# A Fourier filter and memory attention on one core: low parts a unit later, a first projection unit without butterflies, triangle zeros split around the maxima, other pacing and load times

## The chip, the core and the metric

The kernel runs on one core of one Trainium2 chip. The metric is device microseconds of one execution. Where the profile speaks of engines, PE is the matrix engine (TensorE), PEld its weight loads, DVE VectorE, ACT ScalarE, POOL GpSimd, and SP the engine that issues most DMAs.

## The reference, cut to what matters

Two unrelated problems share the kernel; their outputs are concatenated.

```
# A: x [1,2048,576], 32 heads of 18, four segments of 512 tokens
q,k,v = heads(x@wq), heads(x@wk), heads(x@wv)
for s in range(4):
    p = softmax(qs@ks.T*18**-0.5 + causal_mask);  a_dot = p@vs
    a_mem = (phi(qs)@M) / (phi(qs)@z + 1e-6)      # memory of earlier segments
    outs.append(g*a_mem + (1-g)*a_dot)
    M += phi(ks).T@vs;  z += sum(phi(ks))
a = concat(outs)@wo
# B: x [1,2048,576]
b = irfft2(rfft2(x) * (w_r + 1j*w_i))
```

## The kernel before, in words

Every engine has one queue, worked off in the order in which the Python code emits instructions; there is no reordering by a scheduler (`manual_schedule`). An instruction that waits holds up all that stands behind it on its engine. Numbers in f32 are split into a high part (a rounded copy) and a low part (the rest), and products are summed over the parts, so that a matmul has companions on ACT (copy of the high part) and DVE (subtraction for the low part).

The program has four stages on PE, which the trace shows one after the other: the forward transform of B, the projections of A, the inverse transform of B, and attention with the output projection.

**Forward transform** (`FFT.forward`). There are 16 units. For a unit u: SP loads `xin` (L114, three buffers); DVE makes sum and difference `eo` (L126, two instructions, two buffers); ACT copies them to the high part `eh` (L129, L130, three fixed tiles); DVE subtracts for the low part `el` (L133). `f1(u)` is 14 matmuls (L145) into one of two PSUM buffers, eight on `eh`, four on `el` and two on a mixed tile, each half starting with four on `eh`. ACT copies the result to `X0` (L150), DVE subtracts for `X1` (L153), and only then is the PSUM buffer free for `f1(u+2)`. `c1(u)` is 12 matmuls (L166) on `X0`, `X1` and a matrix `cfw` that POOL's queue loads (L118, four buffers); ACT copies its result to the array `Z` (L157). In the loop at step u PE gets `f1(u)` and `c1(u-2)`; DVE gets `eo(u+2)`, a subtraction for a projection weight (L429, called `wl` below), `X1(u-1)` and `el(u+2)`. In the first steps `X1` stands ahead of `eo`.

**Projections** (`ATT.projections`). Four segments, each with nine units of queries and keys and four of values. A query/key unit is 14 matmuls of 512 columns (L485) into one of five PSUM buffers `pj`. What follows is a chain over three engines: ACT copies the first bf16 part `sp` (L498), DVE subtracts it from PSUM (L505), ACT copies the second part (L512), PE subtracts that with one matmul (L514, weights `nid`), ACT copies the third part (L515). PE's queue has the L514 of a unit behind the 14 matmuls of the next unit. On DVE and ACT the same stage carries pieces of the middle of the transform: butterflies on `Z` (L230) and twiddles (`tw` on ACT, L239, then L242 on DVE). A counter (`Pace`) hands them out: `take(w)` per unit, with `w` worked out from how many pieces are left.

**Attention** (`ATT.attention`). A step t is one head; four steps make a block k. In step t PE computes the scores of head t+11 once to find row maxima (`s1`, L678, maxima on DVE at L686 and L692), the scores of head t a second time with the maximum subtracted (`s2`, L727 to L736), ACT takes the exponential into `P` (L728, L733, L737), and PE multiplies an earlier block with the values (`pv`, L756: in step 4k+5 the first half of block k, in step 4k+7 the second). The zeros above the diagonal are written by POOL after the block's last head: four `affine_select` instructions at L741, of about 0.6 us each, on the tiles P0, P1 (twice) and P2. The first half of `pv` reads P0 and the last quarter of P1; the second half reads the rest of P1 and P2. `mpath(k+2)` begins in step 4k+4: DVE (L704) and ACT (L705) finish the maxima of a later block, POOL splits them into two bf16 parts `mh` (L707, L708), and one step later PE transposes them (L711, tile `mt`).

The rest of attention's work stands in a background list `bg`: preparation of the output weights (`late_setup`; its subtraction `wol` on POOL is L650), the denominators (`den`), then per segment `mixed` (memory product `pn` at L831, broadcasts `pb` at L837 and L878, their use on DVE at L838, L881, L883, an addition on POOL at L884) and the output projection `oproj` (L901). `pn` and `pb` share one PSUM buffer. `run_bg` is called twice a step, with 0 and with 1.2: it adds the number to an account and runs one piece when the account is at least 1. So at 1.2 every fifth step runs two pieces.

Loads for later steps go through a list `q`, from which a step takes one (every eighth step two). In steps 16 to 20 five tiles `pq` of 252 or 144 KB are loaded as well, for `den` in step 34. ACT's queue issues one small DMA per block, which brings the maxima to the query tile (L717).

Of the kernel before, what the change touches and what calls it, by code (L numbers as in the profile page):

```python
# [5 lines left out]
F32=mybir.dt.float32; F32R=mybir.dt.float32r  # L6
# [96 lines left out]
class FFT:  # L103
# [4 lines left out]
    def forward(s,xp,cp,pp,wl,xs,consts):  # L108
# [3 lines left out]
        def load(u):  # L112
            xin[u]=xp.tile([128,2,3,128],F32,name="xin",bufs=3)
            nc.sync.dma_start(xin[u],io["xb"][u])  # L114
        def loadc(u):
            a,b=BORD[u]
            cw[u]=cp.tile([128,2,384],F32R,name="cfw",bufs=4)
            nc.gpsimd.dma_start(cw[u],io["cfw"][4*a+b].rearrange("p (h m) -> p h m",h=2))  # L118
# [65 lines left out]
        for i in range(2):  # L184
            for x in p: next(x)
        load(3)
        zp=pp.tile([128,2,512],F32,name="f1",tag="f1")
        zeros(26)
        s.pace=Pace(44+124+32)
        for u in range(20):  # L190
            p=prep(u+2) if u+2<16 else iter(())
            if 0<u<17: ev0(u-1)
            if 2<u<18: evz(u-3)
            if 0<u<4: ev1(u-1)
            if u%4==3 and u>6: s.pace.add(s.stage1((u-7)//4))
            next(p,None)
            if 1<u: next(wl,None)
            if 3<u<17: ev1(u-1)
            next(p,None)
            if u<16: f1(u)  # L200
            if u+4<16: load(u+4)
            elif u<18: next(xs,None)
            if 1<u<18: c1(u-2)
            if u==17: evz(15)
            if 0<u<15: loadc(u+1)
            if u>13: s.pace.take(2)
# [201 lines left out]
class ATT:  # L408
# [58 lines left out]
    def first(s,x0,xp):  # L467

        s.xh={};s.xl={}; s.x0=x0
        P=[s.xprep(0,t,x0,xp,[128,2,3,128],"xin",3) for t in range(5)]  # L470
# [100 lines left out]
    def projections(s,xp,tp,pp,wv,pace,hook):  # L571

        live=[]
        s.nid=wv.tile([128,128],BF,name="nid"); s.nc.scalar.activation(s.nid,s.ident,AF.Copy,scale=-1.0)
        lw=s.load_w("wv",576,wv,xp,288,"xl",4)
        def advance():
            for l in list(live):
                try: next(l)
                except StopIteration: live.remove(l)
        tot=pace.left-8  # L580
        for g in range(4):
            if g<3: xq=[s.xprep(g+1,t,(xp,s.x0)[g%2],xp,[128,512],"xst",2) for t in range(5)]
            for i in range(13):
                u=s.qk_unit(g,i,tp,pp) if i<9 else s.v_unit(g,i-9,tp,pp)
                if i==4 and g<3: s.pk=tp.tile([128,4,576],F32,name="pk",bufs=1)
                next(u)
                hook(g,i)
                next(lw,None); next(lw,None)
                if g<3 and i in (4,6,8,10,12): next(xq[(i-4)//2])
                if g<3 and i in (1,3,5,7,9): next(xq[(i-1)//2])  # L590
                w=tot/(36+16*2.4)*(1.0 if i<9 else 2.4)
                advance()
                pace.take(w*.4)
                advance()
                next(u)
                pace.take(w*.6)
                live.append(u)
        while live: advance()
# [34 lines left out]
    def late_setup(s,cp):  # L633
# [4 lines left out]
        for t in (0,1,2,3,5,4,6):  # L638
# [6 lines left out]
            if len(q)>(t<6):  # L645
# [3 lines left out]
                nc.scalar.copy(s.woh[:,u],x)  # L649
                nc.gpsimd.tensor_tensor(s.wol[:r,u],x[:r],s.woh[:r,u].bitcast(F32),op=OP.subtract)  # L650
        yield
# [67 lines left out]
    def s2(s,t):  # L719
# [19 lines left out]
        if hh==3 or k==31 and hh==2:  # L739
            def sel(x):  # L740
                nc.gpsimd.affine_select(out=x[:,r],in_=x[:,r],pattern=[[0,r.stop-r.start],[1,128]],compare_op=OP.is_ge,fill=0.0,base=0,channel_multiplier=-1)  # L741
            sel(P[0][:,:,:128])
            sel(P[1][:,:,:128])
            sel(P[1][:,:,384:])
            sel(P[2][:,:,:128])
        yield
# [94 lines left out]
    def mixed(s,g):  # L841

        c=s.combine(g-1)
        d=5 if g==3 else 4
        for i in range(5+d):
            next(c,None); yield
            if i>=d:
                for _ in s.mem1(g,ORD[i-d]): yield
    def ux_load(s,g,t):
        r=126 if t<4 else 72  # L850
        s.ux[t]=s.tp.tile([128,512],F32,name="ux",tag="ux",bufs=3)
        s.nc.sync.dma_start(s.ux[t][:r],s.uD[g][126*t:126*t+r])
    def combine(s,g):
# [19 lines left out]
        for t in range(7+late):  # L873
            if t>1 and not late: high(ORD[t-2]); low(ORD[t-2])
            if t<5:
# [6 lines left out]
                else:  # L882
                    nc.vector.tensor_tensor(x[:r],x[:r],pb[:r],op=OP.mult)  # L883
                    eng().tensor_tensor(s.am[t][:r],x[:r],s.am[t][:r],op=OP.add)  # L884
                t=i
# [53 lines left out]
    def begin(s,sm,sp,ps1):  # L939
        s.late=[]; s.now=-1  # L940
        s.sm,s.sp,s.ps1=sm,sp,ps1
        s.mh=sm.tile([128,8,16],BF,name="mh",bufs=1); s.nc.gpsimd.memset(s.mh,0.0)
        s.mg={};s.mx={};s.m2={};s.P={};s.vs={};s.rc={};s.am={};s.pq={};s.ux={};s.potag=None
    def prologue(s):
# [20 lines left out]
    def attention(s,tp,ps):  # L965
# [7 lines left out]
        q=[]  # L973
# [11 lines left out]
        for t in range(133):  # L985
            k,hh=divmod(t,4); n,qd=divmod(k,2); g=k//8
            if hh==0 and qd==0:
                if 0<n<14: q+=s.stack_dmas(n+2,0)
                if 0<n<13: q+=s.stack_dmas(n+3,1)
                if n+2<16: q.append(lambda n=n: s.load_v(n+2))  # L990
            st=t%32
            if 16<=t<21: s.pq_load(1,ORD[t-16])
            if t==34: bg.append(s.den(1,lane))
# [187 lines left out]
```

## Time and profile before

| | |
|---|---|
| median of 3 runs | 700.23 us (699.89 to 700.64) |
| the profiled execution | 701.5 us, its span 699.8 us |
| PE busy | 680.0 us (97%), 5040 matmuls |
| DVE, ACT, POOL busy | 537.7 us (77%), 445.3 us (64%), 192.3 us (27%) |
| chain that ended last | PE 83%, DVE 6%, DMA 3%, ACT 3%, POOL 2%, issue 2% |
| granted TensorE clock | 1.00 |
| DMA | 123.81 MB, mean 177 GB/s |

The span is the time from the first to the last instruction of the trace. A row of a timeline gives the start and the length in us, then the engine, the line, the operation, and what it writes and reads; a number in square brackets is the idle time of the engine just before it, with what ended that time. Matmuls are pipelined: one of 512 columns on f32 is shown as some 400 ns long and yet the next starts after some 230 ns, so rows of PE overlap. A row of the waits gives the total in us, how often, and the longest.

### The profile page before, as it was taken

The page shows a single profiled execution, that of the slowest core. Times are in us where ns is not written, and L with a number is a line of the kernel's source. Part 1 is how long each engine was busy: PE and PEld are TensorE (multiplying, and loading weights), DVE is VectorE, ACT ScalarE, POOL GpSimd, SP SyncE. Part 2 cuts the span into 40 slices and gives each one's busy share as a digit, 9 for nine tenths or more (in the row PEclk, how much of TensorE's full clock was granted, in tenths as well). Part 3 has the DMA queues.
Part 4 walks back from the last instruction along what each step waited for, and adds up shares of the span by engine and source line. Part 5 has one row for each costly group of instructions (what it writes and reads, how often), then busy time and mean ns, then how long its engine had stood idle before and what let it go on. Part 6 is the DMA issues. An engine that isn't in the chain of part 4 may idle for free.

```text
span 699.8 us, 14371 instructions
## 1 busy us (share of the span) xinstructions
PE 680.0 (97%) x5040; PEld 501.9 (72%) x5040; DVE 537.7 (77%) x1149; ACT 445.3 (64%) x997; POOL 192.3 (27%) x389
## 2 busy tenths in 40 slices
PE   8999899999999999999999899999999999998998
PEld 5999679879879879999954455445666445663497
DVE  5898989789689679798588788888667876567633
ACT  4786695584684574545387687777656776567531
POOL 2111000100200101665135343443323652235310
PEclk9999999999999999999999999999999999999999
DMA  9895355594465778999348876986666776442142
GB/s 335 279 316 179 111 162 190 154 268 155 130 191 190 171 213 297 206 231 250 130 124 193 182 172 153 197 196 161 148 141 166 200 161 154 101 132 67 29 152 90
DMA packets 71362, 123.81 MB, mean 177 GB/s; under 512 B 12236, under 2 KB 39530, under 8 KB 67698
## 3 DMA queue, kind: packets, MB, share of 16 engines
q1 hardware_dynamic: 64638, 106.89, 58.0%
q0 software_dynamic: 5632, 15.76, 8.3%
q8 instruction: 40, 0.66, 0.4%
q10 hardware_dynamic: 1020, 0.25, 0.2%
q14 instruction: 32, 0.26, 0.1%
HBM read 82.10 MB, written 39.81 MB: 174 GB/s over the span
## 4 chain that ended last, share of the span: by engine, by line
PE 83%; DVE 6%; DMA 3%; ACT 3%; POOL 2%; issue 2%; ACTq 0%; SPq 0%; DVEq 0%; POOLq 0%
PE pj L485 15%; PE s L678 10%; PE pv L756 10%; PE pjv L485 9%; PE po L901 6%; PE i L318 4%; PE i L329 4%; PE s L727 3%; PE f L145 3%; PE s L731 3%; PE c L166 3%; PE po L930 2%; PE s L691 2%; PE pn L831 2%; PE pm L553 2%
## 5 line engine op out<-in xcount | busy, mean ns | idle before, releaser
L686 DVE CUSTOM_DVE_ANT_0 junk<-s,x 128x512 bf16<-128x512 f32 x248 | 137.0, 552 | 56.0 <-PE s L678 50.9
L741 POOL TENSOR_SCALAR_AFFINE_SELECT P<-P 128x512 f32<-128x512 f32 (+2 forms) x132 | 78.2, 623 | 112.4 <-ACT P L728 104.6
L692 DVE TENSOR_REDUCE mx<-s 128x4 f32<-128x512 f32 x128 | 87.7, 685 | 6.2 <-PE s L691 3.9
L728 ACT ACTIVATE P<-s 128x512 f32<-128x512 f32 x128 | 77.9, 609 | 12.3 <-PE s L727 3.4
L756 PE MATMUL pv<-P,vs 128*32 128x512 f32 (+3 forms) x1024 | 82.5, 439 | 0.1
L737 ACT ACTIVATE P<-s 128x256 f32<-128x256 f32 x128 | 50.0, 391 | 46.3 <-PE s L736 46.0
L733 ACT ACTIVATE P<-s 128x512 f32<-128x512 f32 x128 | 77.8, 608 | 2.5 <-PE s L732 2.2
L678 PE MATMUL s<-Ks,Qs 108*128 108x384 bf16 (+3 forms) x256 | 69.2, 301 | 1.5 <-DVE mx L692 1.2
L756 PEld LDWEIGHTS pv<-P,vs 128*32 128x32 f32 x1024 | 26.9, 109 | 45.3 <-issue 34.9
L485 PE MATMUL pj<-x,wqkh 128*128 128x512 f32 x162 | 56.4, 408 | 0.0
L230 DVE TENSOR_TENSOR Z<-Z 128x580 f32<-128x580 f32 (+2 forms) x51 | 45.6, 911 | 0.5
L678 PEld LDWEIGHTS <-Qs 108*128 108x128 bf16 x320 | 31.5, 98 | 19.3 <-issue 9.2
L691 PE MATMUL s<-tri,idb 128*128 128x128 bf16 x256 | 43.0, 219 | 0.0
L543 POOL MEMSET vt<- 128x32 f32 x16 | 2.3, 161 | 139.1 <-PE pm L553 127.8
L318 PE MATMUL i<-civ,Y 128*128 128x256 f32 (+1 forms) x288 | 39.2, 288 | 0.2 <-POOL Y L303 0.2
L318 PEld LDWEIGHTS i<-civ,Y 128*128 128x128 f32 (+1 forms) x288 | 36.6, 181 | 0.9 <-POOL Y L303 0.4
L329 PE MATMUL i<-itab,T 128*128 128x290 f32 (+1 forms) x224 | 36.6, 306 | 0.1
L485 PEld LDWEIGHTS pj<-x,wqkh 128*128 128x128 f32 x162 | 30.4, 189 | 8.5 <-issue 2.0
L485 PE MATMUL pj<-xh,wqkl 128*128 128x512 f32 x90 | 35.6, 395 | 0.0
L485 PE MATMUL pj<-xh,wqkh 128*128 128x512 f32 x90 | 35.6, 395 | 0.0
L485 PE MATMUL pj<-x,wqkl 128*128 128x512 f32 x90 | 35.5, 395 | 0.0
L504 DVE SCALAR_TENSOR_TENSOR ex<-pj,ex 128x512 f32<-128x512 f32 (+1 forms) x28 | 19.3, 689 | 20.2 <-ACT ex L502 20.1
(216 smaller groups left out, 1805.9 us busy)
## 6 DMA issues: line engine op xcount, KB each, us to landing
qkD<-sp SPq DMA_DIRECT2D x32, 384.0 KB
xin<-xb SPq DMA_DIRECT2D x16, 384.0 KB
cfw<-cfw POOLq DMA_DIRECT2D x16, 384.0 KB, 5.5
civ<-civ POOLq DMA_DIRECT2D x16, 384.0 KB, 9.7
vs<-vD SPq DMA_DIRECT2D x16, 330.0 KB
vD<-vt SPq DMA_DIRECT2D x16, 311.0 KB
W<-w SPq DMA_DIRECT2D x16, 290.0 KB
yb<-yout SPq DMA_DIRECT2D x16, 290.0 KB
```

Source lines behind the costliest of these rows:

```text
L318: nc.tensor.matmul(p[:m,k],Y[i][:,q,c*128:c*128+m],cc[:,hl,o:o+256],start=n==0,stop=n==5)
L329: nc.tensor.matmul(p,x,t,start=n==0,stop=n==6)
L485: s.nc.tensor.matmul(out,a,b,start=i==0,stop=i==len(L)-1)
L678: nc.tensor.matmul(out,Q[:108,h,128*i:128*i+128],K[:108,h,:128*(i+1)],start=True,stop=True)
L686: nc.vector.tensor_tensor_reduce(out=junk[:,:w],in0=src,in1=s.mask[:,512-w:],scale=1.0,scalar=-3.0e38, op0=OP.add,op1=OP.max,accum_out=s.m ...
L691: nc.tensor.matmul(pa[:,o+w-128:o+w],s.idb,s.tri,start=False,stop=True,skip_group_check=True)
L692: nc.vector.tensor_reduce(out=s.mx[k][:,hh],in_=pa.rearrange("p (b c) -> p b c",c=128),axis=mybir.AxisListType.X,op=OP.max)
L728: nc.scalar.activation(P[0][:,hh],p0,AF.Exp,scale=SC)
L733: nc.scalar.activation(P[1][:,hh],p1,AF.Exp,scale=SC)
L737: nc.scalar.activation(P[2][:,hh],p2,AF.Exp,scale=SC)
L741: nc.gpsimd.affine_select(out=x[:,r],in_=x[:,r],pattern=[[0,r.stop-r.start],[1,128]],compare_op=OP.is_ge,fill=0.0,base=0,channel_multiplie ...
L756: nc.tensor.matmul(s.pvt[32*hh:32*hh+32,128*j:],vt[:,j,19*h:19*h+32],mv[0][:,hh,mv[1]],start=j==0,stop=j>1,skip_group_check=True)
```

## The change

The edits fall in three groups.

- *Forward.* `xin` has four buffers and `cfw` three. In step u DVE now gets `eo(u+2)`, `wl`, `X1(u-1)` and then `el(u+1)`, the low part of the unit made in the step before; in the first steps too `X1` stands ahead of `el`.
- *Projections.* The first unit of the first segment takes no pieces (`w` is 0 there); the others get a little more each, and five pieces instead of eight are left for later.
- *Attention.* POOL writes P0 and the last quarter of P1 in step 4k+3, and P1's first quarter and P2 in step 4k+4 behind the two `mh` instructions. The `wol` subtraction and, in steps of one kind, the addition of `combine` go to the end of their step. The background rate is 1.2 at first, 1.0 while `mixed` of segments 1 and 2 runs, 1.35 after it, and 1.2 from `mixed` of segment 3 on. The five `pq` loads stand in steps 18, 21, 24, 27 and 30; the load of the values is put at place 6 of the list `q` instead of its end.

```diff
-            xin[u]=xp.tile([128,2,3,128],F32,name="xin",bufs=3)
+            xin[u]=xp.tile([128,2,3,128],F32,name="xin",bufs=4)
...
-            cw[u]=cp.tile([128,2,384],F32R,name="cfw",bufs=4)
+            cw[u]=cp.tile([128,2,384],F32R,name="cfw",bufs=3)
...
+        p=[]
...
-            p=prep(u+2) if u+2<16 else iter(())
+            if u+2<16: p.append(prep(u+2))
             if 0<u<17: ev0(u-1)
             if 2<u<18: evz(u-3)
-            if 0<u<4: ev1(u-1)
             if u%4==3 and u>6: s.pace.add(s.stage1((u-7)//4))
-            next(p,None)
-            if 1<u: next(wl,None)
-            if 3<u<17: ev1(u-1)
-            next(p,None)
+            if u>=2:
+                if u<14: next(p[-1])
+                next(wl,None)
+            if 0<u<17: ev1(u-1)
+            if 0<u<15: next(p.pop(0))
+            if u<2: next(p[-1])
             if u<16: f1(u)
...
-        tot=pace.left-8
+        tot=pace.left-5
...
-                w=tot/(36+16*2.4)*(1.0 if i<9 else 2.4)
+                w=tot/(35+16*2.4)*((1.0 if i<9 else 2.4) if g>0 or i>=1 else 0.0)
...
-                nc.gpsimd.tensor_tensor(s.wol[:r,u],x[:r],s.woh[:r,u].bitcast(F32),op=OP.subtract)
+                s.later(1,lambda u=u,x=x,r=r: nc.gpsimd.tensor_tensor(s.wol[:r,u],x[:r],s.woh[:r,u].bitcast(F32),op=OP.subtract))
+                yield
...
             sel(P[0][:,:,:128])
-            sel(P[1][:,:,:128])
             sel(P[1][:,:,384:])
-            sel(P[2][:,:,:128])
+            def rest():
+                sel(P[1][:,:,:128])
+                sel(P[2][:,:,:128])
+            if k<31: s.rest=rest
+            else: rest()
...
+        s.rate=1.0 if g<3 else 1.2
         c=s.combine(g-1)
...
+        if g<3: s.rate=1.35
...
-                    eng().tensor_tensor(s.am[t][:r],x[:r],s.am[t][:r],op=OP.add)
+                    f=lambda t=t,x=x,r=r,e=eng(): e.tensor_tensor(s.am[t][:r],x[:r],s.am[t][:r],op=OP.add)
+                    f() if eng() is nc.vector or s.now%4<3 or g==2 else s.later(1,f)
...
-                if n+2<16: q.append(lambda n=n: s.load_v(n+2))
+                if n+2<16: q.insert(6,lambda n=n: s.load_v(n+2))
             st=t%32
-            if 16<=t<21: s.pq_load(1,ORD[t-16])
+            if t in (18,21,24,27,30): s.pq_load(1,ORD[(18,21,24,27,30).index(t)])
...
-            run_bg(1.2)
+            run_bg(s.rate)
...
             if hh==0 and k+2<32: m=s.mpath(k+2); next(m)
+            if hh==0 and s.rest: s.rest(); s.rest=None
```

Three places show how this moves instructions. The numbers in tile names count allocations. In the changed file lines stand 2 to 9 lower (L431 is the old L429, L507 the old L505, L744 the old L741).

DVE in the forward transform, from the sum and difference of unit 2 on, before: each `el` stands right behind the `eo` of its own unit (`eh` names ACT's copy in between).

```order
L126 TENSOR_TENSOR eo_189<-xin_132 128x384 x2
L133 TENSOR_TENSOR el_194<-eo_189,eh2_114 128x768
L153 TENSOR_TENSOR X1_220<-f1_196,X0_218 128x580
L126 TENSOR_TENSOR eo_222<-xin_160 128x384 x2
L133 TENSOR_TENSOR el_227<-eo_222,eh0_112 128x768
L153 TENSOR_TENSOR X1_250<-f1_229,X0_248 128x580
L126 TENSOR_TENSOR eo_252<-xin_216 128x384 x2
```

And in the changed kernel, from the same instruction on:

```order
L126 TENSOR_TENSOR eo_189<-xin_132 128x384 x2
L153 TENSOR_TENSOR X1_218<-f1_194,X0_216 128x580
L133 TENSOR_TENSOR el_220<-eo_189,eh2_114 128x768
L126 TENSOR_TENSOR eo_222<-xin_160 128x384 x2
L126 TENSOR_TENSOR eo_248<-xin_214 128x384 x2
L153 TENSOR_TENSOR X1_257<-f1_227,X0_246 128x580
L133 TENSOR_TENSOR el_259<-eo_222,eh0_112 128x768
```

Between an `eo` and its `el` there now stand another unit's `eo` and an `X1`; `X1` of unit 1 (X1_257) stands behind the `eo` of units 3 and 4, where it had stood ahead of the latter (X1_250).

ACT at the start of the projections, before; `sp3` are the parts of the first units (1015, 1044, 1087 are units 0, 1, 2), `wvh` a value weight, `tw` the twiddles of a butterfly stage.

```order
L512 CAST sp3_1015<-pj_976 128x512
L498 CAST sp3_1044<-pj_999 128x512
L239 ACTIVATE tw_1046<-Z_94 128x290 x2
L515 CAST sp3_1015<-pj_976 128x512
L239 ACTIVATE tw_1060<-Z_94 128x290 x2
L239 ACTIVATE tw_1064<-Z_94 128x290 x2
L444 CAST wvh_984<-raw_1009 128x288
L444 CAST wvh_984<-raw_1035 128x288
L512 CAST sp3_1044<-pj_999 128x512
```

And in the changed kernel (units 0, 1, 2 are 1013, 1042, 1076), from the second part of unit 1 on:

```order
L514 CAST sp3_1042<-pj_997 128x512
L500 CAST sp3_1076<-pj_1025 128x512
L241 ACTIVATE tw_1078<-Z_94 128x290 x2
L517 CAST sp3_1042<-pj_997 128x512
L241 ACTIVATE tw_1092<-Z_94 128x290 x2
L241 ACTIVATE tw_1096<-Z_94 128x290 x2
L446 CAST wvh_984<-raw_1037 128x288
L446 CAST wvh_984<-raw_1065 128x288
```

The first twiddles have moved from between the parts of unit 1 to between the parts of unit 2 (behind the last row a copy `xh` follows, then the second part of unit 2). On DVE nine L230 instructions stood between the last preparation of x (L464) and the first L505; six do now.

POOL at the first blocks of attention, before: four selects, then the two `mh`.

```order
L741 AFFINE_SELECT P0_4281<-P0_4281 128x4x128
L741 AFFINE_SELECT P1_4282<-P1_4282 128x4x128 x2
L741 AFFINE_SELECT P2_4283<-P2_4283 128x4x128
L707 CAST mh_3126<-mg_4312 128x16
L708 TENSOR_TENSOR mh_3126<-mg_4312,mh_3126 128x16
```

And in the changed kernel:

```order
L744 AFFINE_SELECT P0_4281<-P0_4281 128x4x128
L744 AFFINE_SELECT P1_4282<-P1_4282 128x4x128
L710 CAST mh_3131<-mg_4312 128x16
L711 TENSOR_TENSOR mh_3131<-mg_4312,mh_3131 128x16
L744 AFFINE_SELECT P1_4282<-P1_4282 128x4x128
L744 AFFINE_SELECT P2_4283<-P2_4283 128x4x128
L652 TENSOR_TENSOR wol_4298<-ob_4299,woh_4297 128x576
```

Two selects have gone from ahead of the `mh` pair to behind it, in 31 of the 32 blocks.

More of the change, by code (lines that the diff above doesn't have):

```diff
@@ L469, in first @@
         s.xh={};s.xl={}; s.x0=x0
-        P=[s.xprep(0,t,x0,xp,[128,2,3,128],"xin",3) for t in range(5)]
+        P=[s.xprep(0,t,x0,xp,[128,2,3,128],"xin",4) for t in range(5)]
         for a,b in (((0,),()),((1,),()),((2,),(0,)),((3,),(1,)),((4,),(2,)),((),(3,4))):
@@ L942, in begin @@
         s.mh=sm.tile([128,8,16],BF,name="mh",bufs=1); s.nc.gpsimd.memset(s.mh,0.0)
-        s.mg={};s.mx={};s.m2={};s.P={};s.vs={};s.rc={};s.am={};s.pq={};s.ux={};s.potag=None
+        s.mg={};s.mx={};s.m2={};s.P={};s.vs={};s.rc={};s.am={};s.pq={};s.ux={};s.rate=1.2;s.potag=s.rest=None
     def prologue(s):
```

## The prediction

> **What bounds the kernel now.** I read the page first, then the stretches of PE's stages, then PE's waits, and then the timeline around each wait.
>
> ```profile
> PE 680.0 (97%) x5040; PEld 501.9 (72%) x5040; DVE 537.7 (77%) x1149; ACT 445.3 (64%) x997; POOL 192.3 (27%) x389
> ```
>
> PE is the bound: no other engine comes near it, and the chain that ended last is 83% PE. So an edit pays only where PE stands still. The stretches (in order: length, then busy time of PE, PEld, DVE, ACT, POOL) say where that is.
>
> ```profile
> 0.00:28.70 28.70, 25.63 (x152) 19.84 (x153) 18.17 (x33) 14.57 (x28) 6.22 (x17) 1.00 0.94 321
> 28.70:68.60 39.90, 39.90 (x296) 39.72 (x295) 36.33 (x57) 30.67 (x56) 5.92 (x11) 1.00 0.79 250
> 68.60:103.50 34.90, 33.00 (x149) 25.39 (x148) 30.74 (x52) 27.21 (x60) 0.90 (x6) 1.00 0.48 134
> 103.50:350.00 246.50, 246.28 (x1604) 219.03 (x1602) 203.81 (x320) 141.02 (x302) 49.95 (x116) 1.00 0.73 198
> 350.00:665.00 315.00, 304.25 (x2626) 168.24 (x2625) 235.88 (x670) 223.73 (x536) 127.53 (x236) 1.00 0.64 149
> ```
>
> Idle PE is 3.07 us at the start, none in the rest of the forward transform, 1.90 in the first projections, 0.22 in the 246 us from there to attention, and 10.75 in attention; the rest of the 19.8 lies in the last 35 us, which no edit reaches. The change can take from 3.07, 1.90 and 10.75, and from nothing else: no matmul is added or removed. PE's waits name the culprits (total, times, longest).
>
> ```profile
> PE mt L711 <- POOL mh L708: 2.7, 6, 0.8
> PE pj L514 <- ACT sp L512: 1.9, 2, 1.4
> ...
> PE f L145 <- DVE X L153: 0.9, 1, 0.9
> ...
> PE s L678 <- DVE mg L704: 1.0, 1, 1.0
> ...
> PE pn L831 <- DVE am L881: 0.7, 1, 0.7
> ...
> PE pn L831 <- DVE ux L883: 0.6, 1, 0.6
> ...
> PE pb L878 <- DVE am L838: 0.3, 1, 0.3
> ```
>
> **What a wait really costs.** The longest of them, on the timeline, beside a unit that ran without a wait, from the chain:
>
> ```profile
> 76.71 0.40 PE L485 MATMUL pj<-x,wqkh 128*128 128x512 f32 x1
> ...
> 78.51 0.38 PE L514 MATMUL pj<-sp,nid 128*128 128x512 bf16 x1 [1.40 <-ACT sp L512]
> ```
> ```profile
> 83.01 3.27 PE pj L485 x14
> ```
>
> Fourteen matmuls take 3.27 us, 0.23 each, but one is drawn 0.40 long. From 76.71 to 78.51 are 1.80 us, so 1.57 are lost where the idle column says 1.40: each wait costs about 0.16 more than its idle time, and I add that. The Trainium skill ("Perfetto Trace Analysis", section "Tensor Engine Instruction (MATMUL, LD_WEIGHTS)") says that the shown end of a matmul is estimated from its size and not observed. By that alone one could keep to the idle column, and the sum below would be about 2 us smaller (693.9 instead of 692.0 at its end); the start times are observed, so this trace bears out the larger loss.
>
> **Forward: −0.6 us.** The wait to go is this one; the chain shows that unit's fourteen matmuls as 2.17 us long, a later one's as 1.90:
>
> ```profile
> 26.56 0.81 PE L145 MATMUL f<-ftab,eh 128*128 128x290 f32 x4 [0.89 <-DVE X L153]
> ```
> ```profile
> 26.56 2.17 PE f L145 x14
> ...
> 34.08 1.90 PE f L145 x14
> 35.98 1.62 PE c L166 x12
> ```
>
> `f1(5)` waited for the PSUM buffer that `X1(3)` frees, and `X1(3)` stood on DVE behind an `el` that waits for ACT's copies of its own `eo`. With `el` a unit behind, that wait is gone: 0.89, 0.16, and 0.27 for the slow restart, 1.3 at most. But in the first steps `X1(1)` now stands behind one more `eo` pair, and ahead of the `el` that `f1(3)` needs:
>
> ```profile
> 17.35 0.75 DVE L153 TENSOR_TENSOR X<-f,X 128x580 fp32r<-128x580 f32 x1
> 18.02 1.02 DVE L126 TENSOR_TENSOR eo<-xin 128x384 f32<-128x384 f32 x2
> 18.16 0.81 PE L145 MATMUL f<-ftab,eh 128*128 128x290 f32 x4
> ```
>
> `X1(1)` ended at 18.10 and `f1(3)` began at 18.16: no slack, so up to 1.02 us (the pair) returns as a wait two units earlier. Bounds −1.3 and 0; I take the middle. After that PE is gapless to 68.6 before and after, and a unit is 1.90 + 1.62 = 3.52 us. Three `cfw` buffers instead of four: the load starts when `c1(u-2)` ends and is due at `c1(u+1)`, 3 × 3.52 − 1.62 = 8.9 us later. Between 18 and 62 us such loads landed after (least, median, most):
>
> ```profile
> DMA to landing us min/median/max: 3.1/5.4/6.9
> ```
>
> So it costs nothing while 2 us of cover hold. The fourth `xin` buffer only lets a load start earlier.
>
> **First projection: −0.8 us.** The rows around the two waits (1.40 and 0.49, with the hidden part 2.2):
>
> ```profile
> 73.17 3.02 DVE L230 TENSOR_TENSOR Z<-Z 128x580 f32<-128x580 f32 x4
> ...
> 77.15 0.69 DVE L505 TENSOR_TENSOR pj<-pj,sp 128x512 f32<-128x512 f32 x1
> ...
> 77.87 0.58 ACT L512 CAST sp<-pj 128x512 bf16<-128x512 f32 x1 [4.38 <-DVE pj L505]
> 78.35 0.59 ACT L498 CAST sp<-pj 128x512 bf16<-128x512 f32 x1
> ...
> 81.99 0.60 ACT L512 CAST sp<-pj 128x512 bf16<-128x512 f32 x1
> ```
> ```profile
> 84.20 0.62 ACT L456 CAST xh<-xst 128x512 fp32r<-128x512 f32 x1
> ```
>
> L505 of unit 0 stood behind the butterflies. Three L230 fewer are ahead of it now, of 3.02 / 4 = 0.75 us: it runs at about 75, L512 is done near 76, and PE's turn for it comes at 76.9. Both old waits go (in the second, unit 1 had the twiddles on ACT between its L498 and L512). But the order puts those twiddles between the parts of unit 2, and the `xh` copy too. From L498 to L512 ACT took 81.99 − 78.35 = 3.64; with `xh` 4.3, with L512 itself 4.9. PE's turn comes one unit after the first part, 3.27 + 0.23 = 3.5. So 1.4 us of wait return at unit 2: −2.2 + 1.4. Bounds −2.2 (ACT gets the twiddles done in other gaps) and 0. The few pieces that later units gain lie beside a gapless PE with DVE at 204 of 246 us.
>
> **Attention, `mh` ahead of half the zeros: −2.8 us.** One of the six waits:
>
> ```profile
> 366.38 2.40 POOL L741 TENSOR_SCALAR_AFFINE_SELECT P<-P 128x512 f32<-128x512 f32 x4
> ...
> 369.00 0.22 POOL L708 TENSOR_TENSOR mh<-mg,mh 128x16 bf16<-128x16 f32 x1
> ...
> 369.28 0.23 PE L711 MATMUL mt<-idb,mh 128*128 128x128 bf16 x1 [0.38 <-POOL mh L708]
> ...
> 371.87 1.28 PE L756 MATMUL pv<-P,vs 128*32 128x384 f32 x16
> ```
>
> Two selects fewer ahead bring `mh` 2.40 / 2 = 1.2 us forward, more than the longest wait (0.8). The six are 2.7 + 6 × 0.16 = 3.7. Two stay in part: one has no selects ahead of it, and in one block a `wol` now falls between the selects and `mh`. I take −2.8 (bounds −3.7 and −1.5). The two late selects end when the old `mh` pair did, at 369.2, and the second half of `pv` that reads them begins at 371.87: 2.6 us of cover, so free. POOL, 27% busy, hides the deferred additions.
>
> **Attention, loads spread: −1.8 us.** The chain has one load in it, and behind it:
>
> ```profile
> 383.13 7.92 DMA pq<-pqD
> ```
> ```profile
> 391.80 0.60 ACT L728 ACTIVATE P<-s 128x512 f32<-128x512 f32 x1 [2.06 <-PE s L736]
> ...
> 392.44 0.38 PE L727 MATMUL s<-Qs,Ks 110*128 110x512 bf16 x1 [0.46 <-ACT P L728]
> ```
>
> ACT's own DMA issue (L717) stood until the `pq` load of 383.13 landed at 391.05, ACT's queue behind it for 2.06 us, and PE lost 0.46 here and 1.0 more (L678 waiting for L704) two microseconds on; with the hidden parts 1.8. With five loads over 13 steps instead of 5 none should take 7.9 us. Bounds −1.8 and 0 (the last load, now in step 30, late for `den` in step 34).
>
> **Attention, paced pieces: −2.0 us.** In a step with two background pieces:
>
> ```profile
> 469.07 0.38 PE L878 MATMUL pb<-rr,sel 96*126 96x512 bf16 x1
> ...
> 469.88 0.67 DVE L881 TENSOR_TENSOR am<-ux,pb 126x512 f32<-126x512 f32 x1
> ...
> 470.61 1.12 PE L831 MATMUL pn<-pq,Mst 126*126 126x512 f32 x2 [0.73 <-DVE am L881]
> ```
>
> `pn` needs the one buffer that `pb` fills and DVE empties. At 1.0 no step runs two such pieces in segments 1 and 2: the waits of 0.7, 0.6 and 0.3 go, with the hidden part 2.1; I take −2.0 (bounds −2.5 and −0.5). At 1.35 the output projection gets denser, but its pieces are PE's own work. Segment 3 keeps 1.2 and its waits.
>
> **The sum.** −0.6 − 0.8 − 2.8 − 1.8 − 2.0 = −8.0. The profiled execution took 701.5 us (span 699.8 and 1.7 around it), so 693.5; it lies 1.3 above the median of 700.23, on which the forecast stands: 692.2, rounded **692.0**. The bounds add up to −11.8 and −2.0: 688.4 to 698.2.
>
> **Rivals.**
> - *The waits only move* (chance 0.14): with these gone, the next one on the same queue is late by nearly as much, as I already expect at unit 2 and `f1(3)`. For it: DVE and ACT are 75% and 71% busy in attention (235.88 and 223.73 of 315). Against it: the waits are few and each has its own cause. It keeps under 2 us: 698.3 to 700.2, say 699.
> - *Slower, through `cfw`* (0.06): three buffers, 8.9 us of lead. If a load took 10 us, each of some twelve `c1` would be 1.1 us late, 13 us, less the 8 gained: 705. It outweighs the gain from a landing of 9.6 us on. Against it: the longest was 6.9, with DMA engines already 0.79 busy.
> - *More goes* (0.05): waits that I left (recurring ones of 0.2 and the coincidence of two reciprocals) vanish as well, 4 us more: 687.
> - The forecast: 0.75.
>
> **Chances.** A measurement of this kernel tells about 0.2% from no change, 698.8 to 701.6. Faster: 0.75, 0.05, and 0.07 of the first rival, 0.87. Same: its other 0.07. Slower: 0.06. The range reaches below the bounds' low end for part of "more goes" and up to 698.5: 687.5 to 698.5.
>
> **What would show it.** Right: no L514 wait in the first unit of the projections and a wait of 1 to 1.6 us near 84; L711 waiting for L708 under 1 us in total; no `pn` wait in segments 1 and 2; idle PE in 350 to 660 down from 10.8 to about 5. Wrong: waits of `c1` for `cfw`, `den` waiting for `pq`, `pv` waiting for the late selects, or a gap at `f1(3)` above 1.3 us.

## The result, and the profile after

The changed kernel takes **698.41 us** (median of 22 runs, 695.56 to 700.98), the kernel before 700.30 (22 runs); the ratio is 0.9967 (95% interval 0.9956 to 0.9977). By the ratio that is faster by 2.3 us (the medians differ by 1.9), less than a third of the 8.0 forecast; it lies inside the range by 0.1 us only, since the range was wide, and not because the sum was right. The profiled execution took 696.91 us (span 695.2), at the low end of its runs; it is 4.6 below the profiled one of before, which lies 1.3 above its median. So the traces below show where time is won and lost, but more of a gain than was measured. Two runs in a slower state of the chip (one of 1328.7 us among the experiments, and one of 743.8 of the kernel before beside it) are left out of the ratios.

The stretches again (length, busy PE, PEld, DVE, ACT, POOL, granted clock, DMA share, GB/s):

```profile
0.00:28.70 28.70, 26.68 (x162) 21.21 (x163) 20.94 (x38) 16.95 (x32) 5.69 (x16) 1.00 0.93 325
28.70:68.60 39.90, 39.90 (x294) 39.67 (x293) 35.73 (x54) 29.71 (x54) 6.45 (x12) 1.00 0.78 252
68.60:103.50 34.90, 34.47 (x166) 27.00 (x165) 31.61 (x54) 28.87 (x64) 0.90 (x6) 1.00 0.52 147
103.50:350.00 246.50, 244.62 (x1579) 217.43 (x1578) 202.47 (x317) 137.86 (x296) 51.01 (x116) 0.99 0.71 195
350.00:665.00 315.00, 307.55 (x2659) 172.29 (x2658) 235.52 (x670) 224.85 (x538) 126.75 (x236) 1.00 0.63 150
```

Idle PE fell from 1.90 to 0.43 in the first projections and from 10.75 to 7.45 in attention (about 5 was forecast). But the stretch that was gapless, 103.5 to 350, now has 1.88 idle and a clock of 0.99. PE's waits (total, times, longest):

```profile
PE i L320 <- ACT T L357: 1.8, 1, 1.8
...
PE s L681 <- DMA Qs<-reD: 1.2, 1, 1.2
...
PE s L681 <- DVE mg L689: 1.0, 1, 1.0
PE mt L714 <- POOL mh L711: 0.9, 2, 0.6
...
PE pj L516 <- ACT sp L514: 0.4, 1, 0.4
...
PE f L145 <- DVE X L153: 0.3, 1, 0.3
```

The old waits did shrink as forecast (transposes 2.7 to 0.9, projections 1.9 to 0.4, no `pn` or `pb` left). The first two rows are new. The third stands at the same matmul as the 1.0 for L704 in the kernel before (its start was 394.55 and is 391.02): that wait has not gone. How far PE is ahead of before, by the start of the same matmul in both traces (before, after):

| matmul | before | after | lead |
|---|---|---|---|
| last of the forward transform | 63.80 | 62.36 | 1.44 |
| a matmul of the fifth unit of the projections | 87.28 | 84.22 | 3.06 |
| last of the projections | 266.57 | 263.79 | 2.78 |
| inverse transform, 65th | 284.27 | 284.59 | **-0.31** |
| attention, `pv` number 128 | 395.63 | 392.10 | 3.53 |
| `pv` number 384 | 461.52 | 457.82 | 3.70 |
| last `pv` | 663.44 | 659.27 | 4.17 |
| last of all | 696.21 | 691.62 | 4.59 |

So 2.8 us were won by 270 us and 3.1 lost within the next 15; attention then wins 4.5 again. (0.84 of the leads is a load, `ftab`, that landed earlier in this run; no edit touches it.) The loss, on the timeline (DVE, POOL, ACT, PE; start, length):

```profile
275.03 1.44 DVE L232 TENSOR_TENSOR Z<-t 128x580 f32<-128x580 f32 x2
276.39 2.43 DVE L232 TENSOR_TENSOR t<-Z 128x580 f32<-128x580 f32 x2
278.74 0.68 DVE L352 TENSOR_TENSOR T<-i,T 128x512 fp32r<-128x512 f32 x1
```
```profile
276.51 2.73 POOL L305 TENSOR_TENSOR Y<-Z,Y 128x512 fp32r<-128x512 f32 x2 [2.33 <-ACT Y L304]
```
```profile
278.47 0.37 ACT L357 CAST T<-i 99x256 fp32r<-99x256 f32 x1
```
```profile
279.52 1.88 PE L320 MATMUL i<-civ,Y 128*128 128x256 f32 x11 [1.78 <-ACT T L357]
```

PE waits for a PSUM buffer of the inverse transform's first unit. The row names ACT, but its last copy (278.47, 0.37 long) was done at 278.84; what ended last is DVE's L352, at 279.42, queued behind five butterflies. In the kernel before the same DVE instruction started at 279.43:

```profile
279.43 0.69 DVE L350 TENSOR_TENSOR T<-i,T 128x512 fp32r<-128x512 f32 x1
```

So PE came 2.8 us sooner and DVE only 0.7. Two of the butterflies took 2.43 beside POOL's subtraction; the pair before them took 1.44. The Trainium skill ("SBUF — State Buffer", section "Who interferes with whom") says that a DVE instruction with two SBUF inputs contends with a GpSimd instruction that reads SBUF; this row agrees, about 1 us.

Behind the wait the clock halves (windows of 2 us; the 1.00, 0.63 is the granted clock):

```profile
278.00:280.00 2.00, 0.48 (x4) 0.51 (x5) 1.94 (x4) 0.81 (x3) 1.90 (x4) 1.00 0.42 130
280.00:282.00 2.00, 2.00 (x13) 2.00 (x13) 1.03 (x2) 0.36 (x1) 1.92 (x3) 0.63 0.68 195
282.00:284.00 2.00, 2.00 (x11) 2.00 (x10) 1.12 (x2) 1.38 (x4) 0.95 (x2) 0.52 0.49 109
284.00:286.00 2.00, 2.00 (x18) 2.00 (x17) 0.51 (x2) 0.40 (x1) 1.51 (x3) 1.00 0.26 89
```

From start to start the wait is 1.95 long, the matmul behind it comes 0.1 late, and the 15 matmuls in the slow time come every 0.21 to 0.24 us instead of 0.12 to 0.14: 1.5 more. Less the 0.4 that the kernel before waited there, that is the 3.1.

The clock goes with the spread of the runs, but does not explain it: of the 22, 15 have a mean clock of 0.998 or less and a median of 699.3; the 7 others have 696.3. Those are 3.0 apart where the slow matmuls cost 1.5, and the profiled run is one of the 15 and took only 696.9.

### The profile page after: what moved, and what is told of

It reads as the page before. It is cut to its first block, busy times and chain, and to the rows that moved or that the text cites. A ratio compares the mean times of both kernels' runs of the same rounds, so it can differ in the third digit from the quotient of the medians.

```text
span 695.2 us, 14377 instructions
## 1 busy us (share of the span) xinstructions
PE 679.8 (98%) x5040; PEld 503.2 (72%) x5040; DVE 539.0 (78%) x1149; ACT 445.1 (64%) x997; POOL 192.6 (28%) x389
## 4 chain that ended last, share of the span: by engine, by line
PE 86%; DMA 4%; DVE 4%; ACT 2%; issue 2%; POOL 1%; SPq 1%; DVEq 0%; ACTq 0%; POOLq 0%
PE pj L487 15%; PE pv L762 10%; PE s L681 10%; PE pjv L487 9%; PE po L910 6%; PE i L320 5%; PE i L331 4%; PE f L145 4%; PE c L166 3%; PE s L730 3%; PE s L734 3%; PE po L939 2%; PE s L694 2%; PE pn L837 2%; DMA ux<-uD 2%
## 5 line engine op out<-in xcount | busy, mean ns | idle before, releaser
L744 POOL TENSOR_SCALAR_AFFINE_SELECT P<-P 128x512 f32<-128x512 f32 (+2 forms) x132 | 78.9, 621 | 72.2 <-ACT P L731 70.4
```

## The experiments

Each kernel ran beside the kernel before on the same chip; ratios are against that, with 95% intervals. "Low clock" counts runs with a mean granted clock of 0.998 or less; of the kernel before these were 6 of 130. The mean takes in some microseconds behind the last matmul, where the clock falls too (at 693.52 in the trace of the changed kernel); in the kept traces that alone makes 0.999 of 1.00, and a fall during the work makes 0.998 or less. The experiments are called e1 to e18.

### Which half gains

The forward and projection edits alone (e1; attention as before):

```diff
+            if 0<u<17: ev1(u-1)
+            if 0<u<15: next(p.pop(0))
...
+        tot=pace.left-5
```

> The kernel before with the forward and first-projection edits alone; attention is the old one. Theory (the start's gain is handed back where the inverse transform begins): PE is 2 to 3 us ahead at 270 us, then waits 1.5 to 2.2 us for T at the second unit of the inverse transform, with DVE's low part of T queued behind five butterflies, and the granted clock falls to 0.5 for about 3.4 us right behind that wait; so the time is 700.3, within 1 us, no different from before. Rival (my prediction's terms hold, 0.6 and 0.8, and the wait at the inverse transform in the changed kernel comes from something else): 698.9 and no wait over 0.5 us at the inverse transform's start.

Measured: 700.49 (12 runs), ratio 0.9998 (0.9980 to 1.0016). PE led by 1.99 at the last projection and by 0.30 after the inverse transform's start, with this wait:

```profile
PE i L320 <- ACT T L357: 1.9, 1, 1.9
```

The gain of the start is handed back there. But the clock did not fall in this trace, and in only 2 of 12 runs: that part of the theory is weaker than it looked.

The attention edits alone (e2):

```diff
+            if k<31: s.rest=rest
...
+            if t in (18,21,24,27,30): s.pq_load(1,ORD[(18,21,24,27,30).index(t)])
...
+            run_bg(s.rate)
```

> The kernel before with the attention edits alone; forward and projections are the old ones. Theory: attention's gain is about 4.5 us as in the traces (not 6.6), and with the old start there is no long wait at the inverse transform and the clock stays at 1.00: 700.3 - 4.5 = 695.8, so faster than the whole change at 698.4. Rival 1 (attention gives only what the whole change gives, 2 us): 698.3. Rival 2 (prediction's terms): 693.7.

Measured: 698.53 (12 runs), 0.9964 (0.9948 to 0.9980), low clock 3. So 2.5 us: as much as the whole change, and 4.1 short of my 6.6. Rival 1 has the time. The trace ends 5.1 ahead of that of the kernel before; but it is of the fastest of the twelve runs, and where the others lose time it does not show.

### The start of the inverse transform

The changed kernel with the old handing-out of pieces (e3):

```diff
-        tot=pace.left-5
+        tot=pace.left-8
...
-                w=tot/(35+16*2.4)*((1.0 if i<9 else 2.4) if g>0 or i>=1 else 0.0)
+                w=tot/(36+16*2.4)*(1.0 if i<9 else 2.4)
```

> The changed kernel with the first-projection edit undone (pieces from the first unit on, eight left for later); forward and attention edits stay. Theory A (the edit of the pieces shifts DVE's order at the inverse transform, one piece more and a collision with POOL): the wait for T falls to 0.3 to 0.6 us, the clock stays at 1.00, the two waits of the first unit come back (2.2): 698.4 + 1.6 - 3.1 = 696.9 or less. Theory B (any lead of PE over DVE is handed back there): PE's lead is only 1.4 us, the wait shrinks to about 0.5 to 1.2 us, and the time is 697 to 698.5.

Measured: 697.60, 0.9952 (0.9935 to 0.9969), low clock 3 of 12. The lead was 1.03 at the last projection and 0.04 in the inverse transform; the waits there were 0.3 each for T and for Y. The time is in theory B's range, the wait in theory A's. But the lead was lost all the same, with the butterflies handed out as in the kernel before: so the few moved pieces are not what takes it, and what PE is ahead of DVE is given up there, as theory B has it.

With more pieces handed out (e4):

```diff
-        tot=pace.left-5
+        tot=pace.left+6
```

> The changed kernel with eleven more pieces handed out during the projections, so that one butterfly instead of five stands between the last split of Y and the low part of T on DVE. Theory: DVE reaches T 3 us earlier, PE does not wait there, the clock stays at 1.00: 698.4 less the wait of 1.9 and the slow clock's 1.7, 694.5 to 695.5. Rival (DVE has no room for them earlier, the pieces only hold up the projections' own chain): new waits of PE for the parts of the projections of 2 to 3 us in all, and 697.5 to 699. Rival on the clock (it falls by chance, not behind the wait): the wait goes, but runs at a mean clock of 0.998 stay as frequent as in the changed kernel, 14 in 22.

Measured: 697.88, 0.9956 (0.9939 to 0.9972), low clock 3 of 11. The wait for T was gone, but PE had nothing to save: its lead of 2.91 at the sixth unit had shrunk to nothing by 267 us, mostly through waits for the parts:

```profile
PE pj L516 <- ACT sp L514: 1.7, 2, 1.0
```

The rival held: handing out more moves the wait into the projections. So I left the number alone and emptied one unit, the last (e12):

```diff
+                if g==3 and i==12: w=0.0
```

> The changed kernel, but the last projection unit takes no butterflies, so none stands on DVE between the last split of Y and the low part of T; the five follow where the fifth Y is split. Theory: the wait for T (1.55 to 1.9) and the fall of the clock behind it go, PE keeps its lead of 2.5 to 2.8 us into attention: 1.7 to 3 us faster than the changed kernel, 695 to 695.8, with 9 of 12 runs at a mean clock of 0.999 or more. Rival 1 (DVE is the limit and the wait only moves to the fifth Y, some 5 us later): a wait of 1 to 2 us near 290, time as changed. Rival 2 (PE's lead is lost again in attention, where a load sets the time): the lead is there at 350 us and gone by 400 us.

Measured: **695.99** (6 runs, 694.89 to 696.98), 0.9934 (0.9919 to 0.9948), low clock 0. DVE now waits for its input, not PE for DVE:

```profile
274.31 1.09 DVE L305 TENSOR_TENSOR Y<-Z,Y 128x512 fp32r<-128x512 f32 x2
276.49 0.69 DVE L352 TENSOR_TENSOR T<-i,T 128x512 fp32r<-128x512 f32 x1 [1.09 <-ACT T L350]
...
283.98 0.76 DVE L232 TENSOR_TENSOR Z<-Z 128x580 f32<-128x580 f32 x1
...
288.33 0.76 DVE L232 TENSOR_TENSOR Z<-t 128x580 f32<-128x580 f32 x1
```
```profile
268.00:288.00 20.00, 19.93 (x159) 19.58 (x158) 14.34 (x26) 9.30 (x23) 9.18 (x17) 1.00 0.75 233
```

The five butterflies follow one by one (the first two are shown), beside 19.93 us of busy PE in 20. PE's lead of 1.84 at the last projection is 1.93 at the end of the inverse transform, and 5.4 at the end. The same on the old attention (e13, which is e1 with that line):

> The kernel before with the forward and first-projection edits, and no butterflies in the last projection unit; attention is the old one. The front edits alone gained nothing (ratio 0.9998). Theory (their gain was lost at the inverse transform's start alone): with that wait gone the lead of some 2 us reaches the end, 700.7 - 2.0 = 698.7. Rival (the old attention with its late load stands until the load lands, whenever PE comes): the lead is gone by 395 us, 700 to 700.7.

Measured: 698.57 (11 runs), 0.9964 (0.9951 to 0.9978), low clock 0. The front edits are worth nothing without this line and 2.5 us with it. The line alone on the kernel before was not run; there it can save no more than the 0.4 that PE loses at that place.

### The parts of attention, alone and in pairs

POOL's edits alone (e5):

```diff
-            sel(P[2][:,:,:128])
+            def rest():
+                sel(P[1][:,:,:128])
+                sel(P[2][:,:,:128])
```

> The kernel before with POOL's edits alone (half the zeros behind the maxima, the deferred subtraction and additions). Theory (the term of 2.8 is right): the six waits of the transposes for POOL shrink from 2.7 to under 1 us, nothing takes their place, 700.7 - 2.5 = 698.2. Rival (these waits cover others, stack loads and DVE): the waits go and come back as waits of the scores, 699.5 to 700.5.

Measured: 702.76, 1.0029 (1.0016 to 1.0043): **slower by 2 us**, low clock 11 of 12. PE came sooner to a stack whose load was late, stood, and the clock halved behind it (chain, PE's row, windows):

```profile
378.88 5.59 DMA vs<-vD
384.47 0.02 issue
384.49 0.31 SPq L805
384.80 0.04 issue
384.84 7.23 DMA Qs<-reD
```
```profile
392.10 0.59 PE L728 MATMUL s<-Qs,Ks 110*128 110x512 bf16 x1 [3.05 <-DMA Qs<-reD]
```
```profile
392.00:394.00 2.00, 1.90 (x7) 0.72 (x7) 0.71 (x3) 2.00 (x6) 1.22 (x2) 0.50 0.86 164
...
398.00:400.00 2.00, 2.00 (x21) 1.21 (x14) 1.17 (x4) 1.04 (x4) 0.51 (x1) 0.83 0.40 124
```

In SP's queue a `pq` load (L805) stood until the values had landed, and the stack's last load behind it. The rival had the kind, a wait of the scores for a stack's load, but not the size; the theory had neither.

The load edits alone (e6):

```diff
-                if n+2<16: q.append(lambda n=n: s.load_v(n+2))
+                if n+2<16: q.insert(6,lambda n=n: s.load_v(n+2))
...
-            if 16<=t<21: s.pq_load(1,ORD[t-16])
+            if t in (18,21,24,27,30): s.pq_load(1,ORD[(18,21,24,27,30).index(t)])
```

> The kernel before with the load edits alone (five loads over 13 steps, the values' load further ahead in the list). Theory: only ACT's stall of 0.46 us at 392 us goes; the wait of 1.0 us two microseconds later belongs to the scores of a new stack and stays, so 0.6 us: 700.1. Rival 1 (prediction's term of 1.8): 698.9 and neither wait. Rival 2 (the values' load now stands ahead of a stack's last load, which lands later): one or two waits of the scores of 1 to 1.5 us at the first head of a stack are new, 701 to 702.

Measured: 698.79 (11 runs, 697.92 to 699.54), 0.9972 (0.9962 to 0.9983), low clock 0. Both waits at 392 and 394 us were gone: rival 1, my prediction's term, was right, and my theory after the result wrong.

The rates alone (e7):

```diff
-            run_bg(1.2)
+            run_bg(s.rate)
```

> The kernel before with the background rates alone. Theory: the three waits of the memory product and of the broadcasts go (2.1 with their hidden part), but most of it is lost again where the rate is 1.35 and at the end, so 0.5 us: 700.2. Rival (prediction's term of 2.0): 698.7. Rival on the other side (pieces come too late and the output projection queues up at the end): 701.5 with a longer last 35 us.

Measured: 703.59 (8 runs), 1.0038 (1.0023 to 1.0054), low clock 6. **Slower by 2.7 us.** The background additions fall differently on POOL (timeline of POOL, then PE's waits):

```profile
548.10 1.26 POOL L886 TENSOR_TENSOR am<-ux,am 72x512 f32<-72x512 f32 x1 [5.75 <-DVE ux L885]
549.32 2.39 POOL L741 TENSOR_SCALAR_AFFINE_SELECT P<-P 128x512 f32<-128x512 f32 x4
551.68 1.26 POOL L886 TENSOR_TENSOR am<-ux,am 126x512 f32<-126x512 f32 x1
```
```profile
PE mt L711 <- POOL mh L708: 5.0, 7, 1.5
```

Four selects and two additions stand ahead of `mh`: the transposes wait 5.0 instead of 2.7. None of the three expectations had that.

POOL's edits with the loads (e9), and then the loads with the rates (e10; the hunks above, together):

```diff
+            def rest():
...
+            if t in (18,21,24,27,30): s.pq_load(1,ORD[(18,21,24,27,30).index(t)])
```

> The kernel before with POOL's edits and the load edits together, old background rate. Alone POOL's edits cost 2 us, because PE reached sooner the place where ACT's issue stands behind the late load and stood there 3.05 us; the loads alone gained 2. Theory (the zeros' gain can only be cashed once the loads are spread): the transposes' waits and the stall at 389 us are both gone, 2.0 + 2.1 to 2.5, so 700.8 - 4.3 = 696.5, and 2 us faster than all attention edits together (698.5): the rates are what costs. Rival (the parts add up: +2.0 and -2.0): 700.8.

Measured: 698.40, 0.9974 (0.9961 to 0.9987). Neither: next to the loads, POOL's edits are worth nothing that can be measured. The transposes' waits shrank from 2.7 to 0.7, and PE stood at the first scores of a new stack instead:

```profile
391.27 0.32 PE L679 MATMUL s<-x,Qs 108*128 108x384 bf16 x1 [1.45 <-DMA pq<-pqD]
```

The `pq` load that the row names had been issued only 0.57 us before (at 390.70), so what ended this wait is not sure. It is the matmul that waited 1.01 in the kernel before and waits 0.96 in the changed one, where the rows name DVE.

```diff
+            if t in (18,21,24,27,30): s.pq_load(1,ORD[(18,21,24,27,30).index(t)])
...
+            run_bg(s.rate)
```

> The kernel before with the load edits and the new background rates, POOL's order the old one. Theory (the new rates cost 2.7 alone because denser background work delays the maxima on POOL and DVE, waits of the transposes of 1.4 us each at 551 and 640 us): these waits are there again, 700.8 - 2.0 + 2.0 = 700.8 or a little more. Rival (the rates cost only by the old load times, at 393 and 410 us): 697.5 or less.

Measured: 701.45, 1.0013 (1.0001 to 1.0025), low clock 9 of 12; again 5.0 of waits of the transposes. As expected. By their ratios the rates cost 2.9 us on the old POOL order; with POOL's edits (0.9964 with, 0.9974 without the rates) they cost nothing.

### Repeats, and the rates in the whole kernel

The changed kernel once more (e8):

> The changed kernel itself once more, on the same chip and in the same hour as the parts. Theory (the 1.8 us wait for T at the inverse transform makes the clock fall in most runs): at least 6 of 12 runs have a mean clock of 0.998 or less and take some 3 us longer than those at 1.00; the latter 696.3, the median 698.4. Rival (the fall of the clock is a matter of the chip and the hour, as the front part alone, with the same wait, showed it in only 2 of 12): 2 or 3 of 12, median 696.5 to 697.

Measured: 697.42 (11 runs), 0.9958 (0.9942 to 0.9974), low clock 4. Between the theories. In its trace PE waits at the same place and the clock stays up:

```profile
279.15 2.38 PE L320 MATMUL i<-civ,Y 128*128 128x256 f32 x18 [1.55 <-ACT T L357]
```
```profile
280.00:282.00 2.00, 2.00 (x18) 2.00 (x18) 1.19 (x3) 1.12 (x3) 1.73 (x3) 1.00 0.69 197
```

PE's lead falls from 2.92 to 1.57 there, by 1.35 instead of 3.1: that much the wait takes by itself. With the old rates in the changed kernel (e11):

```diff
-        s.rate=1.0 if g<3 else 1.2
...
-        if g<3: s.rate=1.35
```

> The changed kernel with the background rate at 1.2 throughout, all else as changed. Theory (the new rates cost about 2 us in any company): 696 to 696.5 and faster than the changed kernel's 697.4 to 698.4 by 1.5 to 2. Rival (the rates are worth my 2.0, once POOL and the loads are out of the way): 699.5 to 700.

Measured: 697.39 (8 runs), 0.9957 (0.9939 to 0.9975), low clock 3. Both wrong: no difference. Because falls of the clock blur this pair, the same once more with the empty last unit (e17, the hunks of e11 and of e12), beside e12 again (e18):

> The changed kernel with no butterflies in the last projection unit and the background rate at 1.2 throughout, beside the same kernel with the new rates. Theory (the new rates are worth nothing once the waits at the inverse transform and the clock's falls are out of the comparison: the four waits of the memory product and the broadcasts, 2.5 us, are traded for waits at new stacks and at the end): within 0.8 of the other, 695.5 to 696.8. Rival 1 (my prediction's 2.0): 698. Rival 2 (the rates cost): 694.5.

> The changed kernel with no butterflies in the last projection unit, once more, as the other side of the comparison of the rates. Theory: 696.0, no run with a mean clock under 0.999. Rival (the six runs of the first time were lucky): some runs at 0.998 or less, median 697 or more.

Measured: 696.08 with the old rates (6 runs, low clock 2) and 696.22 with the new (7 runs, low clock 0), ratios 0.9936 and 0.9933. Both theories held: the rates do nothing here. With the old ones the trace has four waits for `pn` and `pb` (0.7, 0.7, 0.5, 0.3); with the new ones none of these, but at a new stack

```profile
PE s L682 <- DMA Qs<-reD: 1.8, 1, 1.8
```

### The loads of a new stack

Last, loads of the next stack taken from the list earlier: five instead of three in the first two steps of eight. First with POOL's edits and the load edits (e14), then with the load edits alone (e15), then in the best kernel (e16).

```diff
-            if q and t%8==0: q.pop(0)()
+            for _ in range((2,1)[t%8] if t%8<2 else 0):
+                if q: q.pop(0)()
```

> POOL's edits and the load edits as in the run of both, and the loads of the next stack issued a step earlier (four instead of two taken from the list in the first two steps of eight). Theory (the zeros' 2.8 shrank to 0.4 because PE then reaches a new stack before its load has landed, the wait of 1.45 at 389 us): that wait goes, 698.4 - 1.6 = 696.8, and with the one of 0.64 at 565 us up to 2.4 off. Rival (the wait is for DVE's maxima or a slot that PE itself frees, and the load's issue only blocks SP): 698 to 699, wait unchanged.

Measured: 700.17, 0.9995 (0.9982 to 1.0008).

> The load edits alone, with the loads of the next stack issued a step earlier; POOL's order is the old one. Theory: PE comes late to the stack there, since it waits for the transposes (2.7 in all), and no wait for a stack load is left to save: 698.8 as without, within 0.5. Rival (earlier stack loads gain in any company): 697 or less. The difference between this run and the one with POOL's edits is what these are worth when the loads are in time: 2 by the first theory of this pair, 0.4 by the rival.

Measured: 702.72, 1.0026 (1.0014 to 1.0038).

> The changed kernel with no butterflies in the last projection unit and the next stack's loads a step earlier. Theory: the waits of the scores of 1.65 at 388 us and 0.85 at 562 us go, 696.0 - 2.5 = 693.5, no run with a mean clock under 0.999: then the forecast's 8 us were there but for two places. Rival (earlier loads collide with the spread loads and the values): 696 or more.

Measured: 696.04 (6 runs), 0.9935 (0.9920 to 0.9951), low clock 0: no better than e12, so the rival held.

In e14 and e16 no wait stands at 389 and 563 us any more, but PE does not come through sooner: the matmul that waited 1.45 in e9 starts at 391.34 in e14 and at 391.27 in e9, and at 389.44 in e16 and 389.46 in e12. PE had lost the time just before, at a wait that came in all three. So these runs do not show that the wait at 389 us was for a load. In e16 (chain; ACT's queue; PE):

```profile
371.11 7.74 DMA x<-qkD
...
378.92 0.62 ACTq L721
```
```profile
379.59 0.60 ACT L732 ACTIVATE P<-s 128x512 f32<-128x512 f32 x1 [1.20 <-PE s L695]
...
380.24 0.38 PE L731 MATMUL s<-Qs,Ks 110*128 110x512 bf16 x1 [1.17 <-ACT P L732]
```

ACT's own issue now stands behind the early load, as `pq` held it before the change. The level of both theories was wrong (by their ratios the earlier loads cost 1.5 and 3.8 us). The difference of e14 and e15, 2.2 us by their ratios, speaks for the first: POOL's edits are worth about that where no wait at the stack follows. What else the early loads cost was not followed further.

## Why the prediction was wrong, point by point

- *What bounds it.* PE, rightly. But "The change can take from 3.07, 1.90 and 10.75, and from nothing else" left out that it can give back where PE had no idle. **This failed first**: I let PE's lead run on to the end at its full size and put what DVE would do to it at nothing, "beside a gapless PE with DVE at 204 of 246 us". That is a mean. The 22 us before the inverse transform needs DVE, in the kernel before:

```profile
257.00:279.00 22.00, 22.00 (x156) 20.89 (x156) 21.10 (x32) 11.68 (x28) 4.02 (x15) 1.00 0.82 275
```

  DVE was 21.1 of 22 busy there, so a PE that comes sooner waits for it. The missing term is 2.4 by e13 against e1 (0.9964 and 0.9998), and 1.7 to 2.3 by the ratios of e12 and of the two series of the changed kernel. In the changed kernel a part of it is the clock: its runs at 0.999 and more have medians of 696.3 and 697.0, only 0.3 and 1.0 behind e12.
- *Forward, -0.6.* Right in kind: the wait at `f1(5)` went, 0.29 came at `f1(3)`, `cfw` landed in 5.2 us in the median and no `c1` waited. Of the trace's lead of 1.44, 0.84 is the landing of `ftab`; 0.60 is left, as forecast, and from the end of unit 1 to the end of unit 15 the eleven traces with these edits all win 0.59 to 0.64. The middle of two bounds was a lucky choice: in the changed kernel 1.0 was lost up to the end of `f1(3)`, as the one bound had it, and 1.6 won from `f1(4)` on, more than the 1.3 of the other.
- *First projection, -0.8.* It was 1.6. Both waits went. At unit 2 I forecast 1.4 and 0.43 came: ACT took 4.32 from the first part to the second, as worked out, but PE's turn (83.08 less 0.43) came 4.5 us behind the first part, not 3.5. PE's queue has the matmul L516 behind the fourteen of the next unit and seven of the one after it (`passes` yields after seven), not behind the fourteen alone as I had written:

```profile
78.13 0.59 ACT L500 CAST sp<-pj 128x512 bf16<-128x512 f32 x1
...
82.45 0.58 ACT L514 CAST sp<-pj 128x512 bf16<-128x512 f32 x1
...
83.08 0.38 PE L516 MATMUL pj<-sp,nid 128*128 128x512 bf16 x1 [0.43 <-ACT sp L514]
```

  Front edits together, with the long wait gone: 2.5 (e13), against 1.4.
- *Loads, -1.8.* 2.0 (e6), and right alone. But the second of its two waits, 1.0 at the first scores of a new stack, is there again in e9 (1.45), in e2 (1.63) and in the changed kernel (0.96); that the two were one cause is not shown.
- *Zeros, -2.8.* Alone +2.0, beside the loads about 0. The waits did go; but they had been covering others: a stack's load in e5 (3.05), the wait of 1.45 in e9 whose end is not sure, and at 563 us in the changed kernel a stack's load again, in its chain:

```profile
556.83 7.10 DMA Qs<-reD
```

  **The second step that failed**: I checked that the late selects had cover, and not what PE would reach sooner.
- *Rates, -2.0.* Alone +2.7, in the whole kernel 0. I removed the three waits from the sum and did not follow the additions on POOL (e7), nor what the stack at 562 us would cost (1.8 in e18, no wait in e17).
- *Rivals.* "The waits only move" (0.14, 698.3 to 700.2) is what happened, at the inverse transform and at new stacks, which I did not name; the time 698.41 lies in it. I held against it that each wait has its own cause. The cause of what comes next need not be the same. Slower through `cfw`: no sign of it.
- The sum: front 2.5 and attention 2.5, less what was lost at the inverse transform, 2.4: about 2.6, and 2.3 is measured. The missing 5.7 of 8.0 are that 2.4 and attention's 4.1, less 1.1 that the front gave more, and 0.3 that stays open. Of attention's 4.1, the parts say only that the zeros and the rates gave 0.5 beside the loads where 4.8 was forecast; which wait takes how much in a run of middle length no trace shows. (The lower bounds add up to -11.5, not -11.8; nothing else hangs on that.)

The best version is e12, a line away: 695.99, and 696.22 when repeated; e16 and e17 are level with it.

## What to carry to other kernels

Before a wait is counted as gained, look at what the waiting engine reaches next, and read the other engines' busy time in that stretch alone: a mean of 204 in 246 hid 21 in 22. Where edits meet in one queue, price them in pairs: two that cost 2.0 and 2.7 us alone cost nothing beside the third. And where a stage ends, leave the last unit free of background work, if what follows needs that engine at once.

## What was not expected of the hardware

The granted clock fell to 0.50 within about 1 us of the end of some waits of PE and stayed there for some 3.4 us (idle 1.78 in the changed kernel, 1.48 in e10, 1.47 in e7), and for 7 us around the end of the 3.05 of e5. Before the last matmul it fell nowhere else in the kept traces. It did not fall behind 1.89 in e1, 1.63 in e2, 1.55 in e8 or 1.78 in e18, so the length alone does not decide, and what does is not shown; low clocks came in 6 of 130 runs of before, 19 of 33 of the changed kernel, 11 of 12 of e5, none of 13 of e12 and its repeat. The Trainium skill ("TensorE: Matmul & The Clock Gate", section "HAM oscillation — how this bites in real kernels") asks for no idle gap over about 3.4 us; by these traces 1.5 to 1.8 can be enough.
